# Fused attention and gated feed-forward kernel: one VectorE transpose for both exponential tiles of a unit, placed behind both maxima

## The chip, the cores and the metric

The kernel runs on one core of a Trainium2 chip, in one launch. The metric is the device time in microseconds of that core from start to end; lower is better. The engines are named by their roles: TensorE (PE) for matmuls, with its weight loads shown apart (PEld), VectorE (DVE), ScalarE (ACT), GpSimd (POOL), and SyncE (SP), which here only issues transfers.

## The reference

Three layers follow each other. Only the first is touched by the change.

```python
# attention: batch 2, 8 heads, 768 rows, 64 columns, float32
q_bucket = number formed by the signs of q @ proj      # 6 bits
k_bucket = number formed by the signs of k @ proj
mask = q_bucket[..., :, None] == k_bucket[..., None, :]
scores = where(mask, q @ k.T / sqrt(64), -1e9)
attn = exp(scores - max(scores))
out = attn / (sum(attn) + 1e-9) @ v
# gated layer: 1536 tokens of 512, hidden 1536
x = (x @ w_a) * (x @ w_b) @ w_out
# experts: top 1 of 8, hidden 1024
out[mask_e] = gate * (relu(x @ w1[e]) @ w2[e])
```

## The kernel before, in words

The first 220 us or so are attention. It walks over 8 pairs of heads, 2 heads in a pair and 3 groups of 256 query rows in a head: 48 units, numbered u = 0 to 47 (`units`, L191; `NU`, L282). The 256 rows of a unit are two halves t = 0 and 1 of 128 rows.

What is done with one half: `scores` (L197) puts a tile of 128 x 768 scores into PSUM with eight matmuls; those of L208 add a large number where the buckets agree, so that the mask needs no operation of its own. There are two such PSUM tiles in all. `rowmax` (L210) takes the negated row maximum on VectorE. `expo` (L215) forms the exponential on ScalarE, with row sums in an accumulator that is read by an instruction of its own, and frees the PSUM tile. Per unit, `recip` (L221) inverts both sums on VectorE, and `normal` (L225) scales both exponential tiles on GpSimd: two small comparisons, one small product, and L232 once per half. `turn` (L234) transposes 32 x 32 blocks of one half on VectorE into the tile `ET` of its head. `pv` (L241) multiplies half of a head's 24 blocks with v on TensorE, 96 small matmuls, into four PSUM banks `pvb`. `epilogue` (L266) copies these sums out on ScalarE, two copies per call. The finishing steps `finish_add`, `finish_high` and `finish_low` (L270 to L280) add two partial sums and split the result into a rounded part and a remainder; the first and the last run on GpSimd.

Each engine takes its instructions in the order of the program, which the loop at L315 writes out by hand. In the pass for unit u stand, in this order: maximum of half 0 of u; scores of half 1 of u; exponential of half 0; scores of half 0 of u+1; reciprocal and normalisation of u-1; transpose of half 0 of u-2; maximum of half 1 of u; transpose of half 1 of u-2; exponential of half 1; and last the 12 blocks of sums of a head that is complete, in two passes out of three. In the third pass (s = 2) TensorE instead prepares a later pair in the same PSUM banks: `turned` (L111) transposes the raw q and k, `signs` (L148) multiplies with proj. ScalarE copies these out (`preps`) in the pass behind, and SyncE then moves halves of q and k between partitions (`swap`, L101) and loads the next raw pair (`load`, L82; one buffer). `load_v` (L89) fetches v two heads ahead. A head's sums are taken in passes 3h+6 and 3h+7 and copied out in 3h+8.

`hook` (L1102) slips other work into the passes. `places` (L1084) gives for each of six weight jobs the passes of its seven steps, which convert the gated layer's first weights on VectorE, ScalarE and GpSimd; `fill` (L1098) gives the passes in which TensorE works on the gated layer's first products (`gated_products`, L534), each a half of 6 matmuls, 16 halves in all. After attention come the gated layer's groups (`gated_out`, L573, is its second product) and the experts.

Of the kernel before, what the change touches and what calls it, by code (L numbers as in the profile page):

```python
# [8 lines left out]
F32 = mybir.dt.float32  # L9
# [16 lines left out]
class Kernel:  # L26
# [37 lines left out]
    def attention(self, xh, xl, pools, hook):  # L64
# [7 lines left out]
        NB32 = S // 32  # L72
        H2 = S // 2
        for tag, shape, dt, n in (
            ("et", [128, NC * S], F32, 2), ("e", [128, S], F32, 6), ("vr", [128, NC * 256], F32, 2), ("raw", [128, 2 * S], F32, 1),
            ("q", [128, S], F32, 2), ("qs", [128, S], F32, 2), ("k", [128, S], F32, 2), ("ks", [128, H2], F32, 2),
            ("xp", [128, S], F32, 2), ("co", [128, S], F32, 2), ("qf", [128, H2], BF16, 2), ("qg", [128, H2], BF16, 2), ("kf", [128, S], BF16, 2), ("sk", [128, H2], BF16, 1),
        ):
            sb.tile(shape, dt, tag=tag, name=tag, bufs=n)
# [135 lines left out]
        def expo(u, t):  # L215
            if t == 0:
                SU[u] = small("su")
            e = E[u, t] = sb.tile([128, 2, H2], F32, tag="e", name="e", bufs=6)
            nc.scalar.activation(e, ST.pop((u, t))[:, :, :H2], AF.Exp, bias=NM[u][:, t:t + 1], accum_out=SU[u][:, t:t + 1])  # L219

        def recip(u):  # L221
            R[u] = small("r")
            nc.vector.reciprocal(R[u], SU.pop(u))

        def normal(u):  # L225
            c, f, r = small("mc"), small("mk"), small("s2")
            nm = NM.pop(u)
            nc.gpsimd.tensor_scalar(f, nm, BIG / 2, 1.0, ALU.is_lt, ALU.mult)
            nc.gpsimd.tensor_scalar(c, nm, BIG / 2, 1.0 / S, ALU.is_ge, ALU.mult)
            nc.gpsimd.tensor_tensor(r, R.pop(u), f, ALU.mult)  # L230
            for t in range(2):
                nc.gpsimd.tensor_scalar(E[u, t], E[u, t], r[:, t:t + 1], c[:, t:t + 1], ALU.mult, ALU.add)  # L232

        def turn(u, t):  # L234
            i, j, g = units[u]
            h, c = 2 * i + j, 2 * g + t
            if c == 0:
# [76 lines left out]

        for u in range(NU + 2):  # L315
            i, r = divmod(u, 6)
            s, w = u % 3, u - 2
            act, last, tr = u < NU, 0 <= u - 1 < NU, w >= 0
            done, fin = divmod(u - 11, 6) if u >= 11 else (-1, 0)
            new = len(pairs)  # L320
            if u == 1 or s == 2 and r == 5:
                new, kind = 1 if u == 1 else (u + 7) // 6, turned
            elif u == 3 or s == 2 and u > 2:
                new, kind = 1 if u == 3 else i + 1, signs
            fresh = []
            if act:
                rowmax(u, 0)
                scores(u, 1)
            moves = [((u - 8) // 3, g) for g in (1, 0)] if s == 2 and u >= 8 else []
            for m in moves[:2 if u == NU - 1 else 1]:  # L330
                epilogue(*m)
            if moves and new < len(pairs):
                fresh.append(kind(new, 1))
            if act:
                expo(u, 0)
            for m in moves[2 if u == NU - 1 else 1:]:
                epilogue(*m)
            masks()
            for prep in preps:
                prep(nc.scalar)  # L340
            if preps and held_kind is turned and held + 1 < len(pairs):
                load(held + 1)
            preps = []
            if u + 1 < NU:
                scores(u + 1, 0)
            if last:
                recip(u - 1)
                normal(u - 1)
            if tr:
                turn(w, 0)  # L350
            hook(u, 3)
            if act:
                rowmax(u, 1)
            if tr:
                turn(w, 1)
            if act:
                expo(u, 1)
            if new < len(pairs):
                preps, held, held_kind = fresh + [kind(new, x) for x in (1, 0)[len(fresh):]], new, kind
            elif s < 2 and u >= 6:  # L360
                pv((u - 6) // 3, range(12 * s, 12 * s + 12))
            hook(u, 0)
            if s == 1 and u >= 7 and (u - 1) // 3 < 2 * len(pairs):
                load_v((u - 1) // 3)
            hook(u, 1)
            if done == len(pairs) - 2:
                for g in range(3):
                    if fin == 2:
                        finish_add(done, cols[g])
            else:  # L370
                for start, step, args in finish:
                    done, fin = divmod(u - 11 - start, 6)
                    if fin == 0 and 0 <= done < len(pairs) - 2:
                        step(done, *args)
            hook(u, 4)
        end = len(pairs) - 1
        for g in (1, 0):
            epilogue(2 * end, g)
# [4 lines left out]
        finish_high(end - 1, slice(0, S))  # L383
        hook(NU + 2, 4)
        hook(NU + 3, 0)
        pv(2 * end + 1, range(12, NB32))
# [659 lines left out]
def tile_kernel(ctx, tc, q, k, v, proj, w_a, w_b, w_out, emb, tau, w1, w2, out, dbg=None):  # L1046
# [5 lines left out]
    with tc.manual_schedule():  # L1052
# [15 lines left out]
        with tc.tile_pool(name="conv", bufs=1, side="left") as X.conv, \  # L1068
# [7 lines left out]
            def late():  # L1076
# [18 lines left out]
            first = [(t, f, w, h) for t in range(2) for f in range(2) for w in range(2) for h in range(2)]  # L1095


            fill = {41: 2, 44: 2, NU: 2, NU + 2: 2, NU + 3: 2, NU + 4: 6}  # L1098

            held = []  # L1100

            def hook(u, at):  # L1102
                if at == 3:
# [202 lines left out]
```

## Time and profile before

| what | us |
|---|---|
| three runs | 738.21, 735.63, 736.68 |
| their median | 736.68 |
| the profiled execution, device time | 740.01 |
| its span in the trace | 738.1 |

A trace shows the span of one execution: from its first to its last instruction. The device time holds about 2 us beside it. Rows of the trace give start, duration, engine, line of the kernel, operation, and output and input by the program's names (st: scores, nm: negated maximum, e: exponential, et: its transpose, r: reciprocal, pv: the sums' PSUM banks, xp and co: sums copied out, vr: v). A bracket behind a row tells how long the engine stood idle before it and what ended the wait; `xN` at its end counts like instructions drawn together. A row of a group ends with its busy us and the mean ns of one, then the idle time before its instructions with what ended most of it. A row by stretch has the stretch, its length, and each engine's busy us with its count of instructions. A row of the waits has who waited for whom, the us in total, how often, and the longest. The mean granted TensorE clock of the span is 0.994 of full speed.

### The profile page before, as it was taken

How to read it: one execution, taken by the hardware profiler on the slowest of the kernel's cores; microseconds unless marked ns; L12 is line 12 of the kernel's file. 1: busy time of each engine (PE TensorE's matmuls, PEld its weight loads, DVE VectorE, ACT ScalarE, POOL GpSimd, SP SyncE). 2: the span in 40 equal slices, each digit the busy share in tenths (PEclk: the TensorE clock that was granted, in tenths of full speed). 3: DMA queues.
4: the chain of work that ended last, by engine and by line, in shares of the span. 5: the costliest groups of instructions: out<-in, count | busy, mean ns of one | idle time of the engine just before them, and what ended most of it. 6: DMA issues, size and time to landing. Idle time of an engine off the chain costs nothing.

```text
span 738.1 us, 16439 instructions
## 1 busy us (share of the span) xinstructions
PE 706.0 (96%) x6793; PEld 584.3 (79%) x6793; DVE 458.5 (62%) x669; ACT 356.7 (48%) x657; POOL 441.7 (60%) x453
## 2 busy tenths in 40 slices
PE   7799999999989999999999999999999999999996
PEld 4356555555658999999999999998888999889995
DVE  3888988988885654655545536434744855555650
ACT  4677887877674333221221221234436655556551
POOL 1666998988786472662745646634513866556651
PEclk9899999999999999999999999999999999999999
DMA  6954566456233230230311111254250957666510
GB/s 151 189 122 111 135 153 140 93 116 138 50 76 108 76 121 27 63 109 6 110 58 58 57 58 58 105 168 155 66 178 30 293 197 241 222 217 239 208 61 23
DMA packets 68605, 88.31 MB, mean 120 GB/s; under 512 B 28963, under 2 KB 41123, under 8 KB 68528
## 3 DMA queue, kind: packets, MB, share of 16 engines
q1 hardware_dynamic: 64320, 79.49, 37.8%
q0 software_dynamic: 2560, 7.34, 2.6%
q8 instruction: 54, 0.88, 0.5%
q10 hardware_dynamic: 1648, 0.39, 0.3%
q14 instruction: 23, 0.19, 0.1%
HBM read 75.52 MB, written 7.34 MB: 112 GB/s over the span
## 4 chain that ended last, share of the span: by engine, by line
PE 79%; DVE 5%; ACT 5%; issue 4%; DMA 3%; POOL 3%; SPq 0%; POOLq 0%; DVEq 0%; ACTq 0%
PE ab L551 24%; PE yp L583 13%; PE op L927 10%; PE hp L877 9%; PE pv L248 8%; PE st L205 5%; ACT e L219 2%; DVE nm L213 2%; PE part L551 2%; PE hr L895 2%; DMA vr<-in_v_dram 2%; DVE et L239 1%; PE st L208 1%; PE xgt L854 1%; POOL e L232 1%
## 5 line engine op out<-in xcount | busy, mean ns | idle before, releaser
L551 PE MATMUL ab<-xh,w 128*128 128x384 f32 x704 | 185.8, 338 | 0.0
L551 PEld LDWEIGHTS ab<-xh,w 128*128 128x128 f32 x704 | 127.7, 188 | 2.0 <-issue 1.2
L566 POOL TENSOR_TENSOR g<-a,g 128x384 fp32r<-128x384 f32 x48 | 57.2, 1191 | 105.8 <-ACT g L565 105.7
L551 PE MATMUL ab<-xl,w 128*128 128x384 f32 x352 | 118.3, 336 | 0.0
L833 POOL TENSOR_TENSOR w<-raw,w 128x1024 fp32r<-128x1024 f32 x36 | 88.0, 2448 | 33.8 <-ACT w L832 32.7
L219 ACT ACTIVATE e<-st,nm 128x768 f32<-128x768 f32 x96 | 86.5, 902 | 40.8 <-DVE nm L213 20.3
L213 DVE TENSOR_REDUCE nm<-st 128x1 f32<-128x768 f32 x96 | 90.2, 941 | 22.7 <-PE st L208 22.6
L583 PE MATMUL yp<-w,g 128*128 128x512 f32 x432 | 102.9, 390 | 0.0
L232 POOL TENSOR_SCALAR e<-e,s,mc 128x768 f32<-128x768 f32 x96 | 95.0, 998 | 5.4 <-POOL s L230 0.2
L239 DVE STREAM_TRANSPOSE et<-e 128x768 f32<-128x768 f32 x96 | 92.3, 963 | 3.9 <-issue 1.5
L205 PE MATMUL st<-ks,qs 64*128 64x384 f32 x192 | 86.5, 531 | 8.2 <-ACT e L219 7.7
L205 PE MATMUL st<-k,q 64*128 64x384 f32 x192 | 86.6, 532 | 7.9 <-ACT e L219 6.9
L583 PEld LDWEIGHTS yp<-w,g 128*128 128x128 f32 x432 | 80.4, 188 | 14.9
L927 PE MATMUL op<-w,hth 128*128 128x512 f32 x256 | 81.0, 397 | 0.1
L877 PE MATMUL hp<-xgh,w 128*128 128x256 f32 x448 | 80.7, 281 | 0.0
L565 ACT CAST g<-a 128x384 fp32r<-128x384 f32 x48 | 24.7, 515 | 104.9 <-DVE a L564 104.9
L248 PE MATMUL pv<-et,vr 32*64 32x192 f32 x3072 | 71.4, 325 | 3.9 <-ACT q L128 1.6
L248 PEld LDWEIGHTS pv<-et,vr 32*64 32x64 f32 x3072 | 59.8, 130 | 19.4 <-issue 9.7
L833 DVE TENSOR_TENSOR w<-raw,w 128x1024 fp32r<-128x1024 f32 x28 | 64.6, 2308 | 14.9 <-ACT w L832 14.9
L877 PEld LDWEIGHTS hp<-xgh,w 128*128 128x128 f32 x448 | 69.1, 188 | 0.3
L560 ACT COPY a<-ab 128x384 f32<-128x384 f32 x44 | 21.0, 478 | 95.1 <-PE ab L551 93.7
L551 PEld LDWEIGHTS ab<-xl,w 128*128 128x128 f32 x352 | 66.2, 188 | 0.8
(202 smaller groups left out, 1244.3 us busy)
## 6 DMA issues: line engine op xcount, KB each, us to landing
raw<-in_moe_w_dram SPq DMA_DIRECT2D x32, 1024.0 KB, 5.3
vr<-in_v_dram SPq DMA_DIRECT2D x64, 192.0 KB, 4.3
raw<-in_moe_w_a_dram SPq DMA_DIRECT2D x5, 1024.0 KB, 5.1
raw<-in_moe_w_b_dram SPq DMA_DIRECT2D x5, 1024.0 KB, 5.0
raw<-in_moe_w_out_dram SPq DMA_DIRECT2D x5, 1024.0 KB, 5.0
raw<-in_k_dram SPq DMA_DIRECT2D x16, 192.0 KB, 4.7
qs<-q SPq DMA_DIRECT2D x16, 192.0 KB, 3.1
ybuf<-y SPq DMA_DIRECT2D x12, 256.0 KB, 6.1
```

The source lines that it names most:

```text
L205: nc.tensor.matmul(st[:, n, :H2], q[d, ql], k[d], start=True, stop=False, tile_position=(64 * n, 0))
L213: nc.vector.tensor_reduce(NM[u][:, t:t + 1], ST[u, t][:, :, :H2], axis=AX.XY, op=ALU.max, negate=True)
L219: nc.scalar.activation(e, ST.pop((u, t))[:, :, :H2], AF.Exp, bias=NM[u][:, t:t + 1], accum_out=SU[u][:, t:t + 1])
L232: nc.gpsimd.tensor_scalar(E[u, t], E[u, t], r[:, t:t + 1], c[:, t:t + 1], ALU.mult, ALU.add)
L239: nc.vector.transpose(ET[h][:, :, c], E.pop((u, t)).rearrange("p a (b s) -> p (a b) s", s=32))
L248: nc.tensor.matmul(pvb[a // 2][m:m + 64, a % 2, :NC * 32], v[d], et[d, n].rearrange("p c s -> p (c s)"), start=(n < 2), stop=(n >= NB32 - ...
L551: nc.tensor.matmul(p[:, :384], w[:, k, fs], x[:, k, cols], start=(k == 0 and n == 0), stop=(k == self.KD - 1 and n == 2),)
L566: nc.gpsimd.tensor_tensor(gl[:, f], a, f32(gh[:, f]), ALU.subtract)
L583: nc.tensor.matmul(p, g[:, f, rows], w[:, f], start=(n == 0), stop=(n == 5))
L833: eng.tensor_tensor(l, raw, f32(h), ALU.subtract)
L877: nc.tensor.matmul(p[:, :256], w[:, k, fs], x[:, k], start=(n == 0), stop=(n == 3 * self.KD - 1))
L927: nc.tensor.matmul(p, h[:, 2 * n + f, rows], w[:, f], start=(n == 0 and f == 0 and m == 0), stop=(n == 3 and f == 1 and m == 2),)
```

## The change

The exponential tile of a unit becomes one tile of two halves (three buffers of double size in place of six), and one VectorE instruction transposes both. In the loop the order of a pass becomes: maximum of half 0 of u; exponential of half 0; reciprocal and normalisation of u-1; maximum of half 1 of u; scores of half 0 of u+1; exponential of half 1; the copies of sums, in passes with s = 1; preparation copies and masks; the transpose of both halves of u-2; scores of half 1 of u+1; then sums or the matmuls of a preparation. A head's sums are taken in passes 3h+5 and 3h+6 and copied out in 3h+7; preparation, v loads and finishing steps move one pass with them. The steps of the weight jobs and six of the fill entries get other passes.

```diff
-("et", [128, NC * S], F32, 2), ("e", [128, S], F32, 6),
+("et", [128, NC * S], F32, 2), ("e", [128, 2 * S], F32, 3),
...
-        def turn(u, t):
+        def turn(u):
...
-            nc.vector.transpose(ET[h][:, :, c], E.pop((u, t)).rearrange("p a (b s) -> p (a b) s", s=32))
+            nc.vector.transpose(
+                ET[h][:, :, 2 * g:2 * g + 2].rearrange("p b c s -> p c b s"),
+                E.pop(u).rearrange("p c (b s) -> p c b s", s=32),
+            )
...
         scores(0, 0)
+        scores(0, 1)
...
+            if u == 1 or r == 4:
+                new, kind = 1 if u == 1 else i + 2, turned
+            elif u == 3 or r == 1:
+                new, kind = 1 if u == 3 else i + 1, signs
             if act:
                 rowmax(u, 0)
+                expo(u, 0)
+            if 0 <= u - 1 < NU:
+                recip(u - 1)
+                normal(u - 1)
+            if act:
+                rowmax(u, 1)
+            if u + 1 < NU:
+                scores(u + 1, 0)
+            if act:
+                expo(u, 1)
+            if s == 1 and u >= 7:
+                for g in (1, 0):
+                    epilogue((u - 7) // 3, g)
             for prep in preps:
                 prep(nc.scalar)
+            masks()
...
+            hook(u, 3)
+            if u >= 2:
+                turn(u - 2)
+            hook(u, 2)
             if u + 1 < NU:
+                scores(u + 1, 1)
             if new < len(pairs):
+                preps, held, held_kind = [kind(new, x) for x in (1, 0)], new, kind
+            elif s != 1 and u >= 5:
+                n = (u - 5) % 3
+                pv((u - 5) // 3, range(12 * n, 12 * n + 12))
             hook(u, 0)
+            if s == 0 and u >= 6 and u // 3 < 2 * len(pairs):
+                load_v(u // 3)
...
             places = (
-                (3, 4, 5, 6, 6, 9, 12), (7, 10, 11, 12, 12, 13, 18), (15, 17, 19, 22, 22, 23, 28), (21, 25, 26, 28, 28, 29, 34),
-                (42, 43, 43, 44, 44, 44, 45),
+                (3, 4, 5, 6, 6, 7, 9), (8, 10, 12, 13, 15, 16, 18), (17, 19, 21, 22, 24, 25, 27), (22, 23, 27, 28, 30, 31, 33),
+                (40, 41, 42, 43, 45, 45, 47),
...
-            fill = {41: 2, 44: 2, NU: 2, NU + 2: 2, NU + 3: 2, NU + 4: 6}
+            fill = {40: 2, 43: 2, 46: 2, NU: 2, NU + 2: 2, NU + 3: 2, NU + 4: 4}
```

## Rows read from the trace of the kernel before

**Rows 1.** The page: busy time, share of the span and instructions of each engine.

```profile
PE 706.0 (96%) x6793; PEld 584.3 (79%) x6793; DVE 458.5 (62%) x669; ACT 356.7 (48%) x657; POOL 441.7 (60%) x453
```

**Rows 2.** Busy us by stretch, TensorE clock, DMA share, GB/s.

```profile
14.00:37.00 23.00, 15.99 (x88) 7.04 (x88) 18.37 (x27) 14.69 (x29) 13.49 (x26) 0.90 0.94 202
37.00:59.70 22.70, 22.16 (x440) 13.79 (x448) 19.78 (x29) 16.43 (x34) 14.95 (x28) 0.95 0.44 103
59.70:158.40 98.70, 92.28 (x1764) 53.12 (x1759) 88.23 (x123) 78.83 (x161) 84.95 (x142) 1.00 0.60 136
158.40:216.80 58.40, 53.82 (x1109) 33.96 (x1100) 50.31 (x71) 42.33 (x88) 47.15 (x81) 1.00 0.35 79
216.80:243.60 26.80, 24.48 (x522) 21.30 (x508) 14.39 (x21) 12.71 (x27) 17.23 (x23) 1.00 0.43 131
```

**Rows 3.** Groups of instructions by line and form, 14 to 226 us.

```profile
L232 POOL TENSOR_SCALAR e<-e,s,mc 128x768 f32<-128x768 f32 x96 | 95.0, 998 | 5.4 <-POOL s L230 0.2
L239 DVE STREAM_TRANSPOSE et<-e 128x768 f32<-128x768 f32 x96 | 92.3, 963 | 3.9 <-issue 1.5 <-POOL e L232 0.9 <-POOL spare L465 0.6
L213 DVE TENSOR_REDUCE nm<-st 128x1 f32<-128x768 f32 x96 | 90.2, 941 | 22.7 <-PE st L208 22.6
L219 ACT ACTIVATE e<-st,nm 128x768 f32<-128x768 f32 x96 | 86.5, 902 | 40.8 <-DVE nm L213 20.3 <-DVE r L223 16.6 <-POOL e L232 2.5
...
L219 ACT ACTIVATION_READ_ACCUMULATOR e<-st,nm 128x1 f32 x96 | 18.7, 195 | 0.0
...
L223 DVE RECIPROCAL r<-su 128x2 f32<-128x2 f32 x48 | 7.2, 150 | 2.5 <-ACT e L219 2.5
```

**Rows 4.** Waits, 14 to 226 us.

```profile
PEld st L205 <- ACT e L219: 42.2, 56, 1.9
...
DVE nm L213 <- PE st L208: 22.6, 29, 2.6
```

**Rows 5.** TensorE in order of time: two blocks of sums, scores between.

```profile
131.98 2.21 PE L248 MATMUL pv<-et,vr 32*64 32x192 f32 x96
...
135.94 1.38 PE L248 MATMUL pv<-et,vr 32*64 32x192 f32 x54
```

**Rows 6.** GpSimd in order of time, 93 to 105 us.

```profile
93.71 1.28 POOL L482 TENSOR_TENSOR w<-spare,w 128x512 fp32r<-128x512 f32 x1
94.94 1.41 POOL L272 TENSOR_TENSOR xp<-xp,co 128x256 f32<-128x256 f32 x2
96.44 0.24 POOL L228 TENSOR_SCALAR mk<-nm 128x2 f32<-128x2 f32 x1
...
99.31 0.72 POOL L272 TENSOR_TENSOR xp<-xp,co 128x256 f32<-128x256 f32 x1
100.12 0.24 POOL L228 TENSOR_SCALAR mk<-nm 128x2 f32<-128x2 f32 x1
```

**Rows 7.** VectorE: first maxima of units 11 and 47, the last transposes.

```profile
59.70 0.95 DVE L213 TENSOR_REDUCE nm<-st 128x1 f32<-128x768 f32 x1
...
216.79 0.92 DVE L213 TENSOR_REDUCE nm<-st 128x1 f32<-128x768 f32 x1
...
222.01 3.63 DVE L239 STREAM_TRANSPOSE et<-e 128x768 f32<-128x768 f32 x4
```

**Rows 8.** SyncE's last load of pair 2, TensorE's transposes of it.

```profile
29.06 2.10 SPq L87 DMA_DIRECT2D raw<-in_q_dram  x1
...
36.92 2.74 PE L114 MATMUL pv<-ident,raw 128*128 128x128 f32 x12
```

**Rows 9.** TensorE behind unit 47: sums, six half-products, output group.

```profile
220.05 2.21 PE L248 MATMUL pv<-et,vr 32*64 32x192 f32 x96 [1.09 <-ACT co L268]
...
237.22 0.45 PE L551 MATMUL part<-xh,w 128*128 128x384 f32 x1
...
243.57 4.24 PE L583 MATMUL yp<-w,g 128*128 128x512 f32 x18
```

More of the change, by code (lines that the diff above doesn't have):

```diff
@@ L74, in attention @@
         for tag, shape, dt, n in (
-            ("et", [128, NC * S], F32, 2), ("e", [128, S], F32, 6), ("vr", [128, NC * 256], F32, 2), ("raw", [128, 2 * S], F32, 1),
+            ("et", [128, NC * S], F32, 2), ("e", [128, 2 * S], F32, 3), ("vr", [128, NC * 256], F32, 2), ("raw", [128, 2 * S], F32, 1),
             ("q", [128, S], F32, 2), ("qs", [128, S], F32, 2), ("k", [128, S], F32, 2), ("ks", [128, H2], F32, 2),
@@ L217, in expo @@
                 SU[u] = small("su")
-            e = E[u, t] = sb.tile([128, 2, H2], F32, tag="e", name="e", bufs=6)
-            nc.scalar.activation(e, ST.pop((u, t))[:, :, :H2], AF.Exp, bias=NM[u][:, t:t + 1], accum_out=SU[u][:, t:t + 1])
+                E[u] = sb.tile([128, 2, S], F32, tag="e", name="e", bufs=3)
+            nc.scalar.activation(halves(E[u][:, t]), ST.pop((u, t))[:, :, :H2], AF.Exp, bias=NM[u][:, t:t + 1], accum_out=SU[u][:, t:t + 1])
         def recip(u):
@@ L231, in normal @@
             for t in range(2):
-                nc.gpsimd.tensor_scalar(E[u, t], E[u, t], r[:, t:t + 1], c[:, t:t + 1], ALU.mult, ALU.add)
-        def turn(u, t):
+                nc.gpsimd.tensor_scalar(E[u][:, t], E[u][:, t], r[:, t:t + 1], c[:, t:t + 1], ALU.mult, ALU.add)
+        def turn(u):
             i, j, g = units[u]
-            h, c = 2 * i + j, 2 * g + t
-            if c == 0:
+            h = 2 * i + j
+            if g == 0:
                 ET[h] = sb.tile([128, NB32, NC, 32], F32, tag="et", name="et", bufs=2)
-            nc.vector.transpose(ET[h][:, :, c], E.pop((u, t)).rearrange("p a (b s) -> p (a b) s", s=32))
+            nc.vector.transpose(
+                ET[h][:, :, 2 * g:2 * g + 2].rearrange("p b c s -> p c b s"),
+                E.pop(u).rearrange("p c (b s) -> p c b s", s=32),
+            )
         def pv(h, blocks):
@@ L316, in attention @@
             i, r = divmod(u, 6)
-            s, w = u % 3, u - 2
-            act, last, tr = u < NU, 0 <= u - 1 < NU, w >= 0
-            done, fin = divmod(u - 11, 6) if u >= 11 else (-1, 0)
+            s, act = u % 3, u < NU
             new = len(pairs)
-            if u == 1 or s == 2 and r == 5:
-                new, kind = 1 if u == 1 else (u + 7) // 6, turned
-            elif u == 3 or s == 2 and u > 2:
+            if u == 1 or r == 4:
+                new, kind = 1 if u == 1 else i + 2, turned
+            elif u == 3 or r == 1:
                 new, kind = 1 if u == 3 else i + 1, signs
-            fresh = []
             if act:
                 rowmax(u, 0)
[L328 to L333, printed above, removed]
-            if act:
[L335 to L338, printed above, removed]
+                expo(u, 0)
+            if 0 <= u - 1 < NU:
+                recip(u - 1)
+                normal(u - 1)
+            if act:
+                rowmax(u, 1)
[6 more added lines that the diff above has]
+                    epilogue((u - 7) // 3, g)
             for prep in preps:
                 prep(nc.scalar)
+            masks()
             if preps and held_kind is turned and held + 1 < len(pairs):
@@ L343, in attention @@
             preps = []
+            hook(u, 3)
+            if u >= 2:
+                turn(u - 2)
+            hook(u, 2)
             if u + 1 < NU:
[L345 to L357, printed above, removed]
+                scores(u + 1, 1)
             if new < len(pairs):
-                preps, held, held_kind = fresh + [kind(new, x) for x in (1, 0)[len(fresh):]], new, kind
-            elif s < 2 and u >= 6:
-                pv((u - 6) // 3, range(12 * s, 12 * s + 12))
+                preps, held, held_kind = [kind(new, x) for x in (1, 0)], new, kind
+            elif s != 1 and u >= 5:
+                n = (u - 5) % 3
+                pv((u - 5) // 3, range(12 * n, 12 * n + 12))
             hook(u, 0)
-            if s == 1 and u >= 7 and (u - 1) // 3 < 2 * len(pairs):
-                load_v((u - 1) // 3)
+            if s == 0 and u >= 6 and u // 3 < 2 * len(pairs):
+                load_v(u // 3)
             hook(u, 1)
-            if done == len(pairs) - 2:
+            if u == NU:
                 for g in range(3):
[L368 to L374, printed above, removed]
+                    finish_add(len(pairs) - 2, cols[g])
+            elif u == NU + 1:
+                finish_high(len(pairs) - 2, slice(0, S))
+            for start, step, args in finish:
+                done, fin = divmod(u - 10 - start, 6)
+                if fin == 0 and 0 <= done < len(pairs) - 2:
+                    step(done, *args)
             hook(u, 4)
         end = len(pairs) - 1
-        for g in (1, 0):
-            epilogue(2 * end, g)
         hook(NU + 2, 0)
@@ L382, in attention @@
         finish_add(end, slice(0, S), slice(0, 64), nc.vector)
-        finish_high(end - 1, slice(0, S))
         hook(NU + 2, 4)
@@ L1095, in tile_kernel @@
             first = [(t, f, w, h) for t in range(2) for f in range(2) for w in range(2) for h in range(2)]
[L1098 removed]
+            fill = {40: 2, 43: 2, 46: 2, NU: 2, NU + 2: 2, NU + 3: 2, NU + 4: 4}
             held = []
             def hook(u, at):
[L1103 removed]
+                if at == 2:
                     while held:
```

## Prediction, made before the changed kernel was run

> **What bounds the kernel now.** I read the page first, then the stretches, the groups of instructions, the waits, and last single units in order of time. The page's first part shows TensorE busy for 96% of the span and VectorE for 62% [rows 1]: over the whole kernel TensorE is the bound. The table by stretch shows that this is not so in attention. From the start to 59.7 us, in the 23 units 11 to 33 (59.7 to 158.4 us) and in the 13 units 34 to 46 (158.4 to 216.8 us) four engines are nearly full together: in the long middle stretch TensorE 92.28 of 98.70 us, VectorE 88.23, GpSimd 84.95, ScalarE 78.83 [rows 2]. A unit takes 98.7 / 23 = 4.29 us there and 58.4 / 13 = 4.49 us later. (A unit is counted from its first maximum; unit 11 begins at 59.70 and unit 47 at 216.79 us [rows 7].) No engine is the bound; the order in which they hand work to each other is. After attention TensorE has almost no gap, so a microsecond saved in attention should move the end by about one.
>
> The waits say how time is lost. Score matmuls stand 42.2 us for an exponential that frees their PSUM tile, and VectorE's maxima stand 22.6 us for scores [rows 3, 4]: the second half's scores are issued only inside their own unit, late for a maximum that comes soon after. For the tiles that GpSimd normalises the transposes wait only 0.9 us [rows 3].
>
> What each engine needs per unit if it never waits, from rows:
> - **TensorE:** two score tiles and a block of sums run back to back in 135.94 - 131.98 = 3.96 us [rows 5]. That is two units in three; the third has transposes or sign products in place of sums.
> - **VectorE:** 88.23 / 23 = 3.84 us, extra jobs included [rows 2].
> - **GpSimd:** a unit's normalisation occupies it from 96.44 to 99.31, 2.87 us; a finishing step from 99.31 to 100.12, 0.81; two adds from 94.94 to 96.44, 1.50; a weight job's step from 93.71 to 94.94, 1.23 [rows 6]. Six units hold 6 x 2.87 + 1.50 + 4 x 0.81 = 22.0 us; the middle 23 units are due 23/6 x 22.0 + 6 x 1.23 = 91.6 us, or 3.98 a unit, and in these rows it runs without a gap. The busy figure hides this, as the short pauses between its instructions are not counted (0.09 us from 100.03 to 100.12).
>
> So a perfect order could bring 4.29 to about 4.0 in the middle, no further.
>
> **The change part by part.**
>
> *One transpose in place of two.* 48 pairs become 48 instructions of 1536 elements. Four separate ones back to back take 3.63 us, with 0.96 for one a step of (3.63 - 0.96) / 3 = 0.89 [rows 3, 7]. The fused one is not in the trace. It can hardly save more than a whole short instruction, the 0.15 us of the reciprocal on two elements [rows 3]; at the other end it saves nothing, as it walks the same addresses. No row is nearer to either end, so I take the middle, 0.08: a step of 1.70 in place of 1.78 us, 4 us of VectorE's time over 48 units, and a gain only where VectorE is late. (The Trainium skill, Perfetto Trace Analysis, Optimizing Scalar/DVE Operations, puts the data-access overhead of a VectorE instruction on SBUF at about 60 ns; by that the estimate is 3 us in place of 4.) A fused instruction that is dearer per element has no row and stays in the slow tail.
>
> *It stands behind both maxima.* In VectorE's queue the unit now reads: maximum, reciprocal, maximum, jobs, turn. The second maximum comes 0.89 us sooner, so the second exponential does too; the turn's 1.7 us then covers the exponentials, and the score tiles that follow them, before the next maximum asks. Queued behind the turn are the next unit's maximum and reciprocal; for these ScalarE and GpSimd wait if the turn is late. It now needs both normalised tiles at about 1.9 us (two maxima and the reciprocal, which overlap a little [rows 3]), where the first transpose needed one tile at about 1 us and the second another at 2.9.
>
> *Scores half a unit sooner.* TensorE now issues both tiles of the next unit, then sums or preparation. The second waits for the second exponential, which ends about 3.1 us into the unit (0.9 maximum, 0.1 reciprocal, 0.9 maximum, 0.9 exponential, 0.2 read of its accumulator, and the hand-overs [rows 3]). Sums behind it begin near 4.1 and end near 6.3, that is, 2.2 into a next unit of 4.1 us, just as that unit's first exponential frees its tile. That fits with almost nothing over. Of VectorE's 22.6 us wait I expect most to go; what is late next is GpSimd.
>
> *Sums and their copies one unit sooner.* The four copies now follow both exponentials and delay the next unit's first by nothing while it has to wait for its maximum. VectorE's first transpose of every third unit no longer stands close behind the sums that free its target. Preparation moves with them: the k and q copies follow the second exponential and hold up the sums of that unit, as they do now. The v loads, the swaps of k and q and the raw loads keep their order in SyncE's queue; v is issued after the same sums and needed five units later, which covers it. At the start this cover is thin: unit 4, not 5, now transposes pair 2, whose last load is still being issued from 29.06 to 31.16 us; today the transposes run at 36.92 [rows 8]. A unit sooner, near 32.5, TensorE would stand for the load with the next scores queued behind: 0 to 4 us, and I take 2. That costs back part of the first gain.
>
> *Jobs and fill moved.* Weight jobs change places at the same total cost. Two half-products move from after the last head to unit 46: six of them took 243.57 - 237.22 = 6.35 us [rows 9], so 2.1 us of TensorE go from the tail into the stage. The cover for the last head's finishing shrinks to four halves and one output group, 4.2 + 4.2 us [rows 9], enough.
>
> **The sum, against this execution (740.0 us, span 738.1; the median of the three runs, 736.7, is 3.3 lower).**
> - Start to 59.7 us: VectorE idles 23.0 - 18.37 = 4.6 us before 37.0 [rows 2], of which half, 2.3, may go; the five units 6 to 10 take 22.7 us, at 4.15 each 20.75, 2.0 less; the load takes back 2 (0 to 4): 2.3 (0.3 to 4.3).
> - Units 11 to 33: a period of 4.15, nearer GpSimd's 3.98 than today's 4.29, as jobs come in bursts: 23 x 0.14 = 3.2 (0 to 7.1).
> - Units 34 to 46: TensorE's 53.82 us plus 2.1 leaves 58.4 - 55.9 = 2.5; at 3.95 a unit it would be 58.4 - 51.4 = 7.0. I take 4.0, nearer the busy time that is a row.
> - Tail, 216.8 to 243.6: 26.80 - 24.48 = 2.3 idle [rows 2], of which 1.09 is a stand of sums behind copies [rows 9], plus the 2.1 moved: 3.5 (2.1 to 4.4).
>
> Together 2.3 + 3.2 + 4.0 + 3.5 = 13.0 us: 740.0 becomes 727.0, the median 736.7 about 723.5. The low ends add up to 4.9 (731.8), the high ends to 22.8 (713.9).
>
> **The rivals.**
> - *The hand-overs were the whole loss.* The period falls to about 4.0 in both stretches: with the high ends at start and tail some 21 us, 716. For it: VectorE's and ScalarE's waits [rows 4]. Against: GpSimd's packed rows [rows 6]. Chance 0.10.
> - *GpSimd paces the stage.* The middle stays near 4.29, and the late stretch gives its 2.5: with little at the start and the tail's moved 2.1 about 5.5 us, 731. For it: 91.6 us of work in 98.7. Chance 0.15.
> - *The change doesn't do what it says:* the sooner scores stand in TensorE's queue until the same exponentials, and its 92.28 us of busy time cannot be packed. Only the tail's idle and the start's would be left, against the new wait for the raw load: within 2 us, 736. Chance 0.07.
> - *Slower: the fused turn waits for the second normalised tile.* Place: VectorE's queue, ahead of the next maximum. Price: one normalisation, 0.998 us [rows 3], less the 0.08 saved. It decides where GpSimd ends later than 1.9 us after the unit's first maximum. If it struck in all 37 units 11 to 47 it would cost 37 x 0.92 = 34 us, against VectorE's present wait of 22.6 / 48 = 0.47 a unit, 17 us, that goes, and 6 us at start and tail: +11, 748. For it: GpSimd's lateness [rows 6]. Against: while VectorE waits, GpSimd already has the next unit's work, so it is not starved, and the loss is only what its own 3.98 us sets. Chance 0.10.
>
> The Trainium skill, in the same section, says that an engine which isn't saturated but makes bubbles on others may finish sooner with its instructions broken up; this change does the reverse. That is the slow rival's rule. The trace speaks against it only in part: VectorE is busy for 89% of the middle stretch, but just 0.9 us of its waits are for the tiles.
>
> **How the numbers follow.** The forecast keeps 0.58. Faster is the forecast, the first two rivals: 0.58 + 0.10 + 0.15 = 0.83; the same 0.07; slower 0.10. By faster and slower I mean over 0.3% (2.2 us), about what a measurement of this kernel can tell from no change. The range, 715 to 733, runs from the sum's high ends to its low ends with both faster rivals in it; the unchanged and slower cases, 0.17, and a little at the fast end lie outside.
>
> **What would show it.** Right: 48 transposes near 1.77 us each; VectorE's wait for scores down from 22.6 to under 10 us; a period near 4.15 in units 11 to 33 with VectorE's turns now and then released by GpSimd; a stand of about 2 us for a raw load before unit 6; the first output group about 13 us sooner than 243.57. Wrong: a fused transpose over 2 us, VectorE's wait for GpSimd above 20 us in total, or sums that start so late that the next unit's scores hold up VectorE as long as before.

## Result, and the profile of the changed kernel

The changed kernel takes 725.8 us (median of 6 runs, 724.0 to 729.3) where the kernel before, on the same chip, takes 738.2 (median of 5, 735.6 to 739.3): a ratio of 0.985 over these runs, with a 95% interval of 0.983 to 0.987. A sixth run of the kernel before, of 3914.92 us, is not counted, and the changed kernel's times go with the granted clock of their runs: 724.0 to 724.7 us at 0.997 to 0.999, but 729.2 (the profiled one) and 729.3 us at 0.993 and 0.992. Six more runs in a later comparison gave 0.986 (0.984 to 0.989). The forecast, 723.5 in a range of 715 to 733 and 13 us below the median, was right in sign and close in size. The closeness is in part luck: two terms were too small, by 6.1 us together, and two too large, by 5.3, and 3.05 us were lost where nothing was forecast.

The profiled execution took 729.2 us with a span of 727.3, 10.8 less than before. The page's first part answers to [rows 1]: VectorE, ScalarE and GpSimd have nearly the busy time that they had, and VectorE 48 instructions fewer; TensorE's, whose ends are modelled, is 10 us less with the same instructions.

```profile
PE 696.2 (96%) x6793; PEld 586.2 (81%) x6793; DVE 457.4 (63%) x621; ACT 354.4 (49%) x657; POOL 439.2 (60%) x453
```

The stretches, cut at the same units as in [rows 2] (a row starts with its bounds and length; then the busy time of TensorE, its weight loads, VectorE, ScalarE and GpSimd, the granted clock, DMA share and GB/s):

```profile
14.00:38.20 24.20, 16.44 (x100) 9.03 (x102) 17.53 (x22) 16.47 (x33) 14.21 (x27) 0.93 0.87 192
38.20:58.50 20.30, 20.24 (x461) 12.49 (x459) 19.90 (x24) 16.43 (x35) 15.81 (x26) 1.00 0.51 122
58.50:150.00 91.50, 86.41 (x1792) 53.89 (x1792) 85.59 (x101) 77.77 (x162) 82.66 (x142) 1.00 0.64 146
150.00:202.20 52.20, 51.78 (x1072) 34.08 (x1069) 48.22 (x57) 40.67 (x87) 47.52 (x81) 1.00 0.38 92
202.20:229.70 27.50, 22.41 (x456) 19.70 (x454) 15.70 (x20) 11.30 (x23) 18.84 (x23) 1.00 0.30 86
```

Unit 6 begins at 38.22, unit 11 at 58.48, unit 34 at 149.96, unit 47 at 202.23, the first output group at 229.72. The row for units 11 to 33 is to be read beside 98.70 us before: 91.5 us, 3.98 a unit; VectorE and GpSimd are busy 2 to 3 us less than in [rows 2] (for GpSimd this is one weight job step and one scaling of a half that fall outside the new bounds), and the stretch is 7.2 shorter: most of what went is their gaps. Units 34 to 46 take 52.3 us, 4.02 each, where they took 58.4. The last row, from unit 47 to the first output group, is 0.7 us longer than in [rows 2], though TensorE has 2.07 us less to do in it.

The groups and the waits, 14 to 215 us (attention, which before lasted to 226), answer to [rows 3, 4]:

```profile
L213 DVE TENSOR_REDUCE nm<-st 128x1 f32<-128x768 f32 x95 | 88.5, 936 | 9.2 <-PE st L208 9.1
...
L239 DVE STREAM_TRANSPOSE et<-e 128x1536 f32<-128x1536 f32 x48 | 85.0, 1772 | 9.0 <-POOL e L232 7.5
```

```profile
PEld st L205 <- ACT e L219: 28.6, 58, 2.1
...
DVE nm L213 <- PE st L208: 9.1, 10, 4.1
...
DVE et L239 <- POOL e L232: 7.5, 10, 1.1
```

VectorE's wait for scores fell from 22.6 to 9.1 us, the score tiles' wait for their exponential from 42.2 to 28.6. What is late in their place is GpSimd: the transposes now wait 7.5 us for its tiles.

GpSimd's own waits show what the late scores had cost. The reciprocal that it needs stands in VectorE's queue behind a maximum, and the maximum waits for scores. Before, GpSimd stood for it in units 11 to 33 (first line) and in units 34 to 46 (second):

```profile
POOL s L230 <- DVE r L223: 5.4, 6, 1.6
...
POOL s L230 <- DVE r L223: 6.9, 8, 1.6
```

In the changed kernel one such wait is left in units 11 to 33, and in units 34 to 46 the profile shows no wait of GpSimd at all:

```profile
POOL s L230 <- DVE r L223: 0.7, 1, 0.7
```

One unit and a half, in order of time, shows who sets the pace:

```profile
109.05 1.95 POOL L232 TENSOR_SCALAR e<-e,s,mc 128x768 f32<-128x768 f32 x2
110.96 1.42 POOL L275 TENSOR_TENSOR xp<-xp,co 128x256 f32<-128x256 f32 x2
112.47 0.24 POOL L228 TENSOR_SCALAR mk<-nm 128x2 f32<-128x2 f32 x1
112.80 0.23 POOL L229 TENSOR_SCALAR mc<-nm 128x2 f32<-128x2 f32 x1
113.10 0.19 POOL L230 TENSOR_TENSOR s<-r,mk 128x2 f32<-128x2 f32 x1
113.40 1.95 POOL L232 TENSOR_SCALAR e<-e,s,mc 128x768 f32<-128x768 f32 x2
115.32 0.73 POOL L275 TENSOR_TENSOR xp<-xp,co 128x256 f32<-128x256 f32 x1
116.14 0.24 POOL L228 TENSOR_SCALAR mk<-nm 128x2 f32<-128x2 f32 x1
```

GpSimd starts the next unit's first small operation (112.47) 0.09 us after its last one of this unit (110.96 + 1.42). No line has an idle note.

```profile
111.03 1.78 DVE L239 STREAM_TRANSPOSE et<-e 128x1536 f32<-128x1536 f32 x1 [0.35 <-POOL e L232]
112.73 0.92 DVE L213 TENSOR_REDUCE nm<-st 128x1 f32<-128x768 f32 x1
...
115.39 1.78 DVE L239 STREAM_TRANSPOSE et<-e 128x1536 f32<-128x1536 f32 x1 [0.81 <-POOL e L232]
```

VectorE's turns at 111.03 and 115.39 are released by GpSimd. A unit takes the 3.98 us that the prediction worked out as GpSimd's floor from [rows 6]; that the hundredth agrees is chance (the stretch holds five weight job steps of the six that were counted, and a stand of 0.7 us).

### The profile page after: what moved, and what is told of

The parts are those of the page before. It is cut to its first block, busy times and chain, and to the rows that moved or that the text cites. A ratio compares the mean times of both kernels' runs of the same rounds, so it can differ in the third digit from the quotient of the medians.

```text
span 727.3 us, 16337 instructions
## 1 busy us (share of the span) xinstructions
PE 696.2 (96%) x6793; PEld 586.2 (81%) x6793; DVE 457.4 (63%) x621; ACT 354.4 (49%) x657; POOL 439.2 (60%) x453
## 4 chain that ended last, share of the span: by engine, by line
PE 70%; POOL 8%; DVE 8%; issue 6%; DMA 5%; ACT 2%; SPq 1%; POOLq 0%; DVEq 0%; ACTq 0%
PE ab L545 25%; PE yp L577 14%; PE op L921 10%; PE hp L871 10%; POOL e L232 4%; PE pv L251 3%; DVE nm L213 3%; PE st L205 2%; DVE et L239 2%; PE hr L889 2%; DMA raw<-in_k_dram 1%; POOL xp L275 1%; DMA vr<-in_v_dram 1%; PE xgt L848 1%; ACT e L219 1%
## 5 line engine op out<-in xcount | busy, mean ns | idle before, releaser
L560 POOL TENSOR_TENSOR g<-a,g 128x384 fp32r<-128x384 f32 x48 | 52.5, 1093 | 105.2 <-ACT g L559 101.9
L239 DVE STREAM_TRANSPOSE et<-e 128x1536 f32<-128x1536 f32 x48 | 85.0, 1772 | 9.0 <-POOL e L232 7.5
L205 PE MATMUL st<-ks,qs 64*128 64x384 f32 x192 | 83.5, 515 | 4.9 <-ACT e L219 4.4
L205 PE MATMUL st<-k,q 64*128 64x384 f32 x192 | 83.8, 517 | 3.7 <-ACT e L219 3.3
```

Of the source, the lines that this page charges most:

```text
L205: nc.tensor.matmul(st[:, n, :H2], q[d, ql], k[d], start=True, stop=False, tile_position=(64 * n, 0))
L239: nc.vector.transpose(ET[h][:, :, 2 * g:2 * g + 2].rearrange("p b c s -> p c b s"), E.pop(u).rearrange("p c (b s) -> p c b s", s=32),)
L560: nc.gpsimd.tensor_tensor(gl[:, f], a, f32(gh[:, f]), ALU.subtract)
```

## The experiments

Diffs are against the changed kernel unless the text says otherwise. "Middle" is the stretch from the first maximum of unit 11 to that of unit 34 (98.7 us before, 91.5 after).

### The fused turn cut in two, both behind both maxima

```diff
-            nc.vector.transpose(ET[h][:, :, 2 * g:2 * g + 2]..., E.pop(u)...)
+            e = E.pop(u)
+            for t in range(2):
+                nc.vector.transpose(ET[h][:, :, 2 * g + t], e[:, t].rearrange("p (b s) -> p b s", s=32))
```

> The changed kernel with the fused transpose cut back into two, both still behind both maxima. Theory (the order of the hand-overs gives the gain, and GpSimd then paces units 11 to 33 at 3.98 us): VectorE has 48 x 0.08 = 4 us more work, nearly all under GpSimd's pace, so 0 to 2 us above the changed kernel's 725.8. Rival 1 (one instruction in place of two is the gain): 8 to 11 us above, near 735. Rival 2 (sums one unit sooner are the gain): no change, 0 to 1 us.

Measured: 724.7 us, 1.1 below the changed kernel where 0 to 2 above was expected; its ratio, 0.982 (0.979 to 0.985), overlaps that of the changed kernel. Its middle takes 90.5 us, with 86.76 us of VectorE's time in it against 85.59 (the window's row): 1.17 us in 23 units, 0.05 a unit, is all that the fusion saves (from start to start two transposes take 1.75 us, 109.55 to 111.30, and the fused one 1.70, 111.03 to 112.73), and none of it reaches the end. The one-instruction form is no part of the gain. The Trainium skill (Perfetto Trace Analysis, Optimizing Scalar/DVE Operations) says that larger operations can raise throughput where the engine is saturated, and that broken-up ones may let work finish sooner where it isn't but makes other engines wait; here the two forms can't be told apart by their times.

### The turns at their old places

```diff
...
+            if u >= 2:
+                turn(u - 2, 0)
             if act:
                 rowmax(u, 1)
...
             if u >= 2:
-                turn(u - 2)
+                turn(u - 2, 1)
```

> The changed kernel with two transposes at the places of before: half 0 ahead of the second maximum, half 1 behind it; scores, exponentials and sums stay where the change put them. Theory (order): the second maximum comes 0.9 us later, with it the second exponential, the second score tile and the sums behind it; the middle period goes from 3.98 back to about 4.2, 5 to 9 us above 725.8 in all. Rival 1 (fusion): about as far above as the run with two transposes behind both maxima. Rival 2 (sums sooner): 0 to 2 us above.

Measured: 734.4 us, ratio 0.995 (0.992 to 0.998), which the theory expected: two thirds of the gain are gone. The middle takes 96.1 us, 4.18 a unit, and VectorE waits for scores again (14 to 222 us):

```profile
PEld st L205 <- ACT e L219: 37.5, 63, 1.8
ACT e L219 <- DVE nm L213: 28.2, 40, 1.3
DVE nm L213 <- PE st L208: 19.3, 26, 2.6
```

With a transpose between the maxima the second exponential, for which the next scores stand, comes that much later. The place behind both maxima is needed.

### The fused turn alone, in the kernel before

Against the kernel before, with the exponential tile of two halves and the second transpose's place kept:

```diff
...
-            if tr:
-                turn(w, 0)
             hook(u, 3)
             if act:
                 rowmax(u, 1)
             if tr:
-                turn(w, 1)
+                turn(w)
```

> The kernel before with one thing changed: one transpose for both halves, at the place where the second one stood, behind the second maximum. Theory (order): as the first transpose leaves its place ahead of the second maximum, that maximum may come 0.9 us sooner, but it waits for scores that are still issued late; 0 to 4 us below the kernel before. Rival 1 (fusion is the gain): 8 to 11 us below. Rival 2 (sums sooner are the gain): within 1 us of the kernel before.

Measured: 749.9 us, ratio 1.017 (1.013 to 1.020): slower, and the expectation missed the sign. The middle takes 104.0 us, 4.52 a unit. Three units' second maxima in VectorE's order show why:

```profile
108.73 0.96 DVE L213 TENSOR_REDUCE nm<-st 128x1 f32<-128x768 f32 x1 [0.51 <-PE st L208]
109.61 1.77 DVE L239 STREAM_TRANSPOSE et<-e 128x1536 f32<-128x1536 f32 x1
...
113.55 0.96 DVE L213 TENSOR_REDUCE nm<-st 128x1 f32<-128x768 f32 x1 [0.72 <-PE st L208]
114.43 1.77 DVE L239 STREAM_TRANSPOSE et<-e 128x1536 f32<-128x1536 f32 x1
...
118.16 0.96 DVE L213 TENSOR_REDUCE nm<-st 128x1 f32<-128x768 f32 x1 [1.05 <-PE st L208]
```

The first transpose had covered the time in which TensorE computes the second half's scores. Without it VectorE stands for them (38.8 us in all, 14 to 222 us, though attention lasts longer here, against 22.6 before), and then turns 1.77 us with the next maximum queued behind. The turn behind both maxima pays only if the scores are there already.

### The scores late again, in the changed kernel

```diff
             if act:
                 rowmax(u, 0)
+                scores(u, 1)
...
-            if u + 1 < NU:
-                scores(u + 1, 1)
```

(and no second scores ahead of the loop).

> The changed kernel with the scores of the second half issued where they were before, behind the first maximum of their own unit; the fused turn behind both maxima and the earlier sums stay. Theory (the turn behind both maxima only pays with the earlier scores): VectorE's wait for scores back above 20 us in the stretch 14 to 215, period of units 11 to 33 at 4.3 to 4.5, time 740 to 752. Rival (the place of the turn and the earlier sums carry the gain, the earlier scores are an extra): within 4 us of the changed kernel, period at most 4.1.

Measured: 801.1 us, ratio 1.087 (1.084 to 1.090). The theory's sign and mechanism hold, its size was far too small: 5.73 us a unit in the middle.

```profile
111.80 0.96 DVE L213 TENSOR_REDUCE nm<-st 128x1 f32<-128x768 f32 x1 [4.36 <-PE st L208]
```

```profile
106.99 3.76 PE L251 MATMUL pv<-et,vr 32*64 32x192 f32 x96 [2.67 <-ACT q L128]
```

The second maximum at 111.80 stood 4.36 us. Ahead of its scores TensorE had a block of sums (3.76 us) that itself stood 2.67 us for ScalarE's copy of q, which follows the second exponential: maximum, exponential, copies, sums and scores had become one chain. TensorE's granted clock in the middle (66.88 to 198.57 us) was 0.95, so a part of the loss is at the lower of its levels (1.2 and 2.4 GHz): the block of sums above took 3.76 us where it takes 2.21 in the changed kernel (216.33).

### The sums one unit later again

Sums, their copies, preparation, value loads and finishing go back by one unit, and the fill to where it was before:

```diff
-            elif s != 1 and u >= 5:
-                n = (u - 5) % 3
-                pv((u - 5) // 3, range(12 * n, 12 * n + 12))
+            elif s != 2 and u >= 6:
+                pv((u - 6) // 3, range(12 * s, 12 * s + 12))
```

> The changed kernel with sums, their copies, preparation, v loads and finishing steps one unit later, as before, and the fill of before; the order of maxima, scores and the fused transpose stays. Theory (order): units 11 to 33 stay at 3.98 to 4.05 us; the stand of 3.8 us for the raw load of pair 2 goes, the tail grows by about 2 us: 722 to 727. Rival 2 (sums sooner are the gain): the middle goes back to 4.2 to 4.3 and the time to 731 to 736.

Measured: 733.0 us, ratio 0.993 (0.990 to 0.996), the middle 97.6 us. The theory's 722 to 727 is missed; the time and the middle, 4.24 us a unit, are those of the second rival, so the earlier sums are needed, though other experiments show that they are not the whole gain. The start behaves as expected (unit 6 at 35.1 instead of 38.2, with no stand for the raw block), but the middle loses 6 us. Two lines show where:

```profile
106.57 2.25 PE L251 MATMUL pv<-et,vr 32*64 32x192 f32 x96
```

```profile
108.94 1.78 DVE L239 STREAM_TRANSPOSE et<-e 128x1536 f32<-128x1536 f32 x1 [1.26 <-issue]
```

A head's first turn writes one of the two transposed buffers, and starts only when the sums of the head two before have read it (106.57 + 2.25 = 108.82). The profile names no releaser in this row, but all eight first turns of the middle stand, 0.99 to 1.26 us each and 9.6 in all, and at 58.43 and 121.94 it names the sums. With the turn behind both maxima this falls late in the unit. A third buffer would separate the two; it was not tried.

### One more small operation on GpSimd in each unit

```diff
             nc.gpsimd.tensor_tensor(r, R.pop(u), f, ALU.mult)
+            nc.gpsimd.tensor_scalar(small("xx"), nm, BIG / 2, 1.0, ALU.is_lt, ALU.mult)
```

> The changed kernel with one more small GpSimd instruction in each unit's normalisation (a third comparison whose result nobody reads, about 0.33 us with its pause). Theory (GpSimd paces units 11 to 33): these 23 units become 23 x 0.33 = 7.6 us longer and part of the rest too, 6 to 13 us above the changed kernel's 725.8. Rival (VectorE or TensorE paces, GpSimd only follows): 0 to 3 us above.

Measured: 737.9 us, ratio 1.001 (0.999 to 1.002): the whole gain is gone. The middle takes 99.1 us, 7.6 more, or 0.33 for each of its 23 units, which is what the operation takes from start to start (110.54 to 110.88):

```profile
110.54 0.24 POOL L231 TENSOR_SCALAR xx<-nm 128x2 f32<-128x2 f32 x1
110.88 1.95 POOL L233 TENSOR_SCALAR e<-e,s,mc 128x768 f32<-128x768 f32 x2
```

The transposes' wait for GpSimd rose from 7.5 us (14 to 215 us) to 18.6 (14 to 222 us). GpSimd paces attention now.

### GpSimd's two comparisons given to VectorE

```diff
-            nc.gpsimd.tensor_scalar(f, nm, BIG / 2, 1.0, ALU.is_lt, ALU.mult)
-            nc.gpsimd.tensor_scalar(c, nm, BIG / 2, 1.0 / S, ALU.is_ge, ALU.mult)
+            nc.vector.tensor_scalar(f, nm, BIG / 2, 1.0, ALU.is_lt, ALU.mult)
+            nc.vector.tensor_scalar(c, nm, BIG / 2, 1.0 / S, ALU.is_ge, ALU.mult)
```

> The changed kernel with the two small comparisons of the normalisation moved from GpSimd to VectorE, behind the reciprocal. GpSimd loses 48 x 0.64 us, VectorE gains 48 x about 0.16. Theory (GpSimd paces): its floor in units 11 to 33 falls from 3.98 to 3.34, VectorE's rises from 3.76 to about 3.92 and is the next to pace, so the middle falls by 0 to 3 us and the time is 721 to 726. Rival (VectorE paces already): 4 to 8 us above 725.8.

Measured: 729.8 us, ratio 0.989 (0.987 to 0.991), no faster than the changed kernel; the expectation missed. The time is at the lower edge of what the rival gave (VectorE paces already, 4 to 8 us above 725.8), but the delay is not in attention: the first output group begins at 229.50, in the changed kernel at 229.72. The middle takes 92.7 us:

```profile
56.49:149.22 92.73, 88.29 (x1794) 54.45 (x1794) 91.57 (x147) 79.89 (x163) 72.32 (x97) 1.00 0.64 144
```

GpSimd falls to 72.32 us and waits; VectorE is busy 91.57 of 92.73 us. A unit takes 4.03 us (92.73 / 23), just above GpSimd's 3.98 without this edit: the bound has moved to VectorE, and the time has not gained. The jobs got dearer besides: the combined mask-and-or on 128 x 512 integers (L448) takes 0.66 us on VectorE in the changed kernel and 0.94 here (means of two from 60 to 145 us).

### The value load of the second head later, at the start

```diff
         load_v(0)
-        load_v(1)
...
                 load(held + 1)
+                if u == 2:
+                    load_v(1)
```

and the second weight piece is fetched in unit 4 instead of ahead of the loop.

> The changed kernel with two early transfers put off: v of head 1 behind the raw load of pair 2, and the second weight piece to unit 4. Theory (TensorE stands 3.8 us for the raw load because those transfers are ahead of it): the stand falls to under 1.5 us, unit 5 from 7.6 to about 4.5 us, and the time to 722 to 724. Rival (the load is issued too late whatever is ahead of it): no change, within 1 us of 725.8.

Measured: 727.1 us, ratio 0.986 (0.984 to 0.988); the expectation missed. The stand for the raw block shrinks from 3.79 to 0.54 us, and the next load in SyncE's queue, the swapped query behind the moved one, takes its place (line 36.23). Unit 6 begins 1.6 us sooner, and the time is the same:

```profile
32.47 0.85 PE L114 MATMUL pv<-ident,raw 128*128 128x128 f32 x6 [0.54 <-DMA raw<-in_q_dram]
...
36.23 0.33 PE L208 MATMUL st<-kf,qg 64*128 64x384 bf16 x1 [1.92 <-DMA qg<-qf]
```

### The tail

VectorE's product of the half-products of pass 48 (L558, which multiplies the two sums of the gated layer) is held until the last turn is issued, and the low parts of the pair before last are finished one pass sooner:

```diff
-                        X.gated_products(0, t, f, w, half, X.part, held if u < NU else None)
+                        X.gated_products(0, t, f, w, half, X.part, held if u <= NU else None)
...
```

> The changed kernel with two things moved behind unit 47: VectorE's product of the fill in pass 48 comes behind the last transpose, not ahead of it, and GpSimd's last three finishing steps of the pair before the last come one pass sooner, away from VectorE's own. Theory (the tail gives back about 2 us, as the last transpose stands 2.4 us behind a product of the fill and the first output group 2.4 us behind VectorE's remainders, which collide with GpSimd's): the stand of the first output group goes, 722 to 724. Rival (these engines are off the path, the output group waits for something else): within 1 us of 725.8.

Measured: 724.9 us, ratio 0.982 (0.981 to 0.984). The first output group begins at 226.41 instead of 229.72 and its stand falls from 2.39 to 0.72 us; the time is 1 us above what was expected, and its interval overlaps that of the changed kernel.

### Start and tail together

The tail's edit, the value load now behind the swapped queries of unit 4, the second weight piece in unit 5:

```diff
             preps = []
             hook(u, 3)
+            if u == 4:
+                load_v(1)
...
-            plan = {(-1, 0): [jobs[0][0], jobs[1][0]], ...
+            plan = {(-1, 0): [jobs[0][0]], (5, 1): [jobs[1][0]], ...
```

> The changed kernel as it is, to stand beside the next run on the same chip: 724 to 727 us, first maximum of unit 6 near 38 us, the first output group near 229.

> Two edits together: the load of the second value block goes out one pass sooner, behind the transposed query loads of that pass and ahead of nothing that unit 5 waits for, and the fill product of pass 48 and the low finish of the pair before last are placed as in the tail experiment. Theory (the 3.79 us that TensorE stood for the raw block and the 2.39 us that the first output group stood for VectorE are time of the kernel): unit 6 near 35 instead of 38.2, the first output group 5 to 6 us sooner than in the changed kernel, in all 719 to 722. Rival (the stretch behind unit 6 is given a start with less work ahead, and gives the gain back by unit 11): unit 11 within 1 us of the changed kernel's 58.5, and only the gain of the tail is left, 723 to 726.

Measured on one chip: the changed kernel 727.9 us, ratio 0.986 (0.984 to 0.989), 1 us above what was expected; this one 720.3 us, ratio 0.979 (0.977 to 0.981), as the theory had it. Unit 6 begins at 34.18, unit 11 at 55.87 (2.6 us sooner than in the profile of the changed kernel; the rest of the 4.0 is given back in units 6 to 10), the first output group at 224.28:

```profile
14.00:34.18 20.18, 15.64 (x102) 8.05 (x104) 17.57 (x24) 15.25 (x31) 13.75 (x25) 1.00 0.80 180
...
55.87:147.37 91.50, 86.43 (x1792) 53.91 (x1792) 85.56 (x101) 77.75 (x162) 82.65 (x142) 1.00 0.63 146
...
199.63:224.40 24.77, 22.41 (x456) 19.78 (x456) 14.42 (x20) 11.47 (x24) 18.09 (x23) 1.00 0.41 127
```

Units 11 to 46 are those of the changed kernel to the hundredth; from unit 47 to the first output group it takes 24.8 us instead of 27.5, and the start is at the full clock. It beats both kernels, and the two intervals of this chip don't overlap.

## Why the prediction was right, and which terms were not

Against the profiled execution of before, the first output group begins 243.57 [rows 9] - 229.72 = 13.85 us sooner, the sum of the first four points; 3.05 of it are lost behind.

- **Start to unit 11: forecast 2.3 us, measured 1.2.** The mechanism was named, and the price was at the high end: the raw load of pair 2 cost 3.79 where I took 2 (0 to 4). Units 6 to 10 took 20.3 us in place of 22.7, as forecast, and the stretch ahead of them 1.2 more.

```profile
34.37 2.79 PE L114 MATMUL pv<-ident,raw 128*128 128x128 f32 x12 [3.79 <-DMA raw<-in_k_dram]
```

  After it the granted clock is 0.64 from 34.3 to 38.2 us, and the same 12 transposes take 2.79 us that take 1.64 when nothing stood before them (start and tail together). (They took 2.74 in [rows 8] too, at a clock of 0.53 behind two stands of 1.33 and 1.25 us, so this part is no loss against before.) With the value load out of SyncE's queue ahead of it, the stand went.
- **Units 11 to 33: forecast 3.2 us (0 to 7.1), measured 7.2.** The floor was right, 3.98 a unit; the step that failed is "a period of 4.15 ... as jobs come in bursts". The floor already held GpSimd's jobs, and its stands for the reciprocal, 5.4 us before, fell to 0.7, so that next to nothing came on top of it. (The same loop took 92.3 us in the tail experiment's profile and 90.5 with the turn cut: the floor is good to some 0.05 a unit.) The second rival named the engine that paces, but left the period near 4.29. The first rival, that the hand-overs were the whole loss, is what happened in this stretch; its 716 us did not follow, because it took the high ends for start and tail.
- **Units 34 to 46: forecast 4.0 (2.5 to 7.0), measured 6.1.** The step that failed is "TensorE's 53.82 us plus 2.1": the moved half-products run behind this stretch (next point), TensorE was busy 51.78 us, and GpSimd, whose stands of 6.9 us are gone, sets the pace here too, at 4.02 a unit.
- **Tail: forecast 3.5 gained (2.1 to 4.4), measured 0.7 lost.** Two steps were wrong. "2.1 us of TensorE go from the tail into the stage" is the first: the moved half-products run from 201.78 to 204.1, all but two of their 12 matmuls behind unit 47's first maximum (202.23), and the stretch holds 72 matmuls of half-products, as before. That TensorE is busy 2.07 us less in it (22.41 against 24.48) comes from sums and scores which now fall before unit 47 begins. Moreover the moved half-products lie in the sums' banks, and the next sums stood 1.46 us until ScalarE, behind the exponentials of unit 47, had copied them out. The second: I took TensorE's present idle time, 2.3 us, as an upper end, and it grew to 5.1, those 1.46 with the two stands below. "The cover ... shrinks ..., enough" did not hold:

```profile
213.34 0.56 DVE L558 TENSOR_TENSOR a<-part,a 128x384 f32<-128x384 f32 x1 [4.40 <-PE part L545]
213.81 1.77 DVE L239 STREAM_TRANSPOSE et<-e 128x1536 f32<-128x1536 f32 x1
213.93 0.51 ACT L559 CAST g<-a 128x384 fp32r<-128x384 f32 x1 [7.91 <-DVE a L558]
...
226.70 2.50 DVE L283 TENSOR_TENSOR xl<-xp,xh 128x384 fp32r<-128x384 f32 x2 [0.58 <-ACT xh L279]
229.12 0.54 DVE L558 TENSOR_TENSOR a<-part,a 128x384 f32<-128x384 f32 x1
```

```profile
206.08 3.82 PE L251 MATMUL pv<-et,vr 32*64 32x192 f32 x170 [1.46 <-ACT a L554]
...
216.33 2.21 PE L251 MATMUL pv<-et,vr 32*64 32x192 f32 x96 [1.02 <-ACT co L271]
...
229.72 1.66 PE L577 MATMUL yp<-w,g 128*128 128x512 f32 x6 [2.39 <-DVE a L558]
```

  The last turn (213.81) could have gone 2.5 us sooner, since GpSimd had finished its tiles at 211.34, but stood behind the product of two half-products (213.34), which itself waited 4.40 us for TensorE. Its cast (213.93) stood 7.91 us in ScalarE's queue ahead of the copies for which the sums at 216.33 waited, and the last product (229.12), for which the output group stood 2.39, came late behind the two subtractions at 226.70. The tail experiment put the product of pass 48 behind the turn, and took three finishing steps away from ahead of those subtractions (last section); the group began 3.3 us sooner, the sums' stand for the copies was gone, and the 1.5 us for the moved half-products stayed.
- **Behind the first output group: forecast 0, measured 3.05 lost,** most of it where a gather feeds the experts. In the profiled execution the gather was issued 10.1 us behind the start of the stores ahead of it (528.14 and 538.20) where it had been 8.1 before (541.84 and 549.91), and TensorE stood for it:

```profile
541.73 0.63 PE L848 MATMUL xgt<-ident,xg 128*128 128x128 f32 x4 [2.03 <-DMA xg<-ybuf,gi]
```

```profile
520.00:545.00 25.00, 22.79 (x162) 20.04 (x162) 10.57 (x41) 9.31 (x17) 4.71 (x4) 0.95 0.47 152
```

  The kernel before shows a clock of 1.00 there and no such stand:

```profile
533.00:557.00 24.00, 23.76 (x178) 20.82 (x177) 11.19 (x42) 10.09 (x18) 5.53 (x5) 1.00 0.55 174
```

  Both profiles of the changed kernel and all of its variants have the stand, with 1.62 to 2.82 us, except the two in which the value load and the second weight piece are moved; the fused turn in the kernel before has none either. What decides it was not settled.
- **The fused turn: forecast 1.77 us each and 0.08 saved a unit, measured 1.772 and 0.05.** The fused step came out at the forecast 1.70 us; two short ones in its place take 1.75, not 1.78. The slow rival's price (it waits for the second normalised tile) is 7.5 us in the waits, but as the prediction argued, GpSimd isn't starved meanwhile, and the period is GpSimd's own.
- **The parts do not add.** I had costed them one by one. By the experiments the three moves need each other: a middle of 4.29 us a unit before, 4.52 with the fused turn alone, 4.18 without its new place, 4.24 without the earlier sums, 5.73 without the earlier scores, and 3.98 with all. Only the turn was tried alone; the earlier scores alone, the earlier sums alone and the new places of the weight jobs were not. The diagnosis that scores come late was right; that the turn at its new place would cost without them was not in the prediction.

## What to carry to other kernels

Where several engines are nearly full together, work out the floor of each from packed rows and take the highest as the new period: with the hand-overs repaired the kernel ran within 0.05 us a unit of it, and a second engine stood so close behind that two small operations, taken from the first and given to it, made it the bound. A step that fills a wait may be moved away only when what was waited for comes sooner; test such moves together, since alone one can look harmful, as the turn did. Work that is moved into another stage has to be looked for there: the half-products ran later than the pass that issued them, and held up the sums whose banks they used. And look at the two ends of a pipeline for themselves: two loads ahead in a queue, one product ahead of a turn and three steps ahead of two subtractions, with what followed behind them, were worth 727.9 - 720.3 = 7.6 us.

## What was not expected of the hardware

A slow neighbour costs more than its wait. Two subtractions of 128 x 384 on VectorE took 2.50 us at 226.70 in the changed kernel: the first 0.96, beside the last of three subtractions that GpSimd ran from 225.11 to 227.25, and the second 1.61, beside a weight job step that came behind these:

```profile
227.21 1.58 POOL L476 TENSOR_TENSOR w<-late,w 128x512 fp32r<-128x512 f32 x1
227.59 1.61 DVE L283 TENSOR_TENSOR xl<-xp,xh 128x384 fp32r<-128x384 f32 x1
```

In the kernel before (239.47) and with start and tail mended (221.57) the two took 1.03, while GpSimd had no instruction under way. The price here was 1.47 us, on the path to the first output group. The Trainium skill (GPSIMD Engine Reference, section 1, Specifications) lists contention between the two engines for SBUF when VectorE reads two inputs there; the rows agree. TensorE's clock, too, adds to a stand: 1.15 us (2.79 against 1.64) on the 12 transposes behind the wait of 3.79 us for the raw block, at a granted clock of 0.50 while they ran (34.37 to 37.16 us).
